# A rarely taken branch two units earlier in layer one, and another order of products in layer two's first step

## The chip, the cores and the metric

One core of one Trainium2 chip. The metric is the device time of one execution in microseconds (us); less is better. The kernel before: 1326.54 us, the median of three runs (1326.3 to 1328.52).

## The reference

Three parts, one after the other. Attention (4 batches, 8 heads, 576 tokens, 64 wide) with a threshold on the scores gives 2304 tokens of 512 values. Then "layer one", a mixture in which each token goes to one of 8 experts, and "layer two", in which each token goes through all 4 experts and the results are weighed:

```python
for e in range(E):                       # layer one, E = 8
    mask = expert_idx == e
    h = np.maximum(xe @ w1[e], 0.0)      # xe = x[mask], 512 -> 1024
    out[mask] = gate_w[mask, None] * (h @ w2[e])
for e in range(E):                       # layer two, E = 4
    h = np.maximum(x @ w1[e], 0.0)
    out += p[:, e:e + 1] * (h @ w2[e])
```

All is fp32. The kernel splits each fp32 operand into a high and a low part and makes three matmuls of the parts (high by high, high by low, low by high), which the helper `three` issues (lines 363 to 368).

## The kernel before, in words

**Layer one** (loop from line 1263) runs 72 units: nine groups of tokens (`j`), for each the four quarters of the first weights (`w == "1"`, `layer1`, line 406) and then the four of the second (`w == "2"`, `layer2`, line 418). A group has a fixed window of columns: 256 tokens of the largest expert first, then the experts by size with windows of 288, 352, 320, 288, 288, 224, 208 and 176. The last two units, 70 and 71, are the third and fourth quarter of the second weights of the last group: 24 matmuls of 176 columns each, then a copy on ACT from PSUM to `y` (line 423). Weights come by transfers on the queue of SP (`fetch`, `fetch2`), and are split into parts by ACT (high) and DVE or POOL (low).

**The branch** (lines 1319 to 1339). An expert with more tokens than its window needs more turns. `rank2` computes on the chip how many there are (`nextra`) and a table of them (`xtab`); the constants of the table, lines 211, 313 and 315, and the loop use `XW`, the columns of one turn. A first turn is made if an expert's tokens exceed its window (`th` is the window plus a multiple of `XW`, from zero up). Behind the last unit every engine loads `nextra` and branches. If there are turns, a loop does them one by one: it loads rows and weights, transposes, computes both products (2 + 8 + 4 = 14 tiles of PSUM, of which the pool `psW` has 8) and copies into `y`; behind the loop `first_part` is made again, since `y` has changed. With no turns nothing of the body runs.

**Layer two** (from line 1343) takes the 2304 tokens in three phases of 768 and makes 16 steps in each, one for a quarter of an expert's hidden columns. A step has a first product `l1` and a second `l2`. `l1` computes a 2 by 2 block product with seven products of blocks, not eight, so it needs sums and differences of blocks of the weights and of `y`. `prep1(j)` makes the weights' blocks for step j: POOL makes four sums (`sx`), `own` splits the blocks that are no sums (products 0, 1 and 2), `made` splits the sums (products 3 to 6); ACT casts the high parts, POOL subtracts for the low ones. `prep2(j)` splits the weights for `l2`. The blocks of `y` lie in parts in `yc[0]` to `yc[6]`; for the first phase `first_part` makes six of them during layer one and leaves the seventh, `yc[2]`, as values in `tt[2]`.

A product `prod(o, m)` (line 1377) is six matmuls of 384 columns, accumulated in the PSUM bank `o`; with `more` it adds to what is there. `add` is on DVE. `relu` makes the high part on ACT and returns the low part's subtraction on DVE, to be called. Within `l1` the order is

```python
prod(X, 0); p1 = copy(X); mid(); prod(Y, 4); q = Y + p1
prod(Z, 5); r = Z + q;    prod(X, 1, True); c11 = relu(0, 0, X)
prod(W, 3); c22 = W + r;  c11(); prod(Z, 2, True); relu(1, 1, c22)()
c21 = Z + q;              prod(W, 6, True); relu(1, 0, c21)(); relu(0, 1, W + q)()
```

with the sums written into PSUM banks. `mid` holds preparations for later steps. In the first step it is `first_blocks` (line 1449): the split of `yc[2]`, then `prep1(1)`'s casts, then `prep2(0)`. The blocks of step 0 (`prep1(0)`) are made at unit 70 (line 1291).

The order of work is the order of the program on each engine: the blocks are under a manual schedule, and an engine takes its instructions strictly in turn. Work of layer two that depends on nothing in the branch, such as POOL's sums for step 1, the load of the tokens' shares and the next transfer of weights, stands before the branch on its queue, since layer two is a second manual block.

Of the kernel before, what the change touches and what calls it, by code (L numbers as in the profile page):

```python
# [11 lines left out]
F32 = mybir.dt.float32  # L12
F32R = mybir.dt.float32r
# [3 lines left out]
ALU = mybir.AluOpType  # L17
# [8 lines left out]

EARLY = 256
WINDOWS = [288, 352, 320, 288, 288, 224, 208, 176]
XW = 256


@with_exitstack
def kernel(
# [309 lines left out]
    def psum():  # L343
        return pools["psum"]()
# [38 lines left out]
    def x_load(row, n, pool, tag, bufs):  # L383
        ts_ = []
        for s in range(0, n, 128):
            m = min(128, n - s)
            X = pool.tile([128, DM], F32, tag=tag, name="xrow", bufs=bufs)
            nc.sync.dma_start(X[:m, :], xs[ds(row + s, m), :])
            ts_.append((X, s, m))
        return ts_  # L390

    def x_tr(X, s, m, xT, pspool):
        ps = pspool()
        for c in range(4):
            nc.tensor.transpose(ps[:, c * 128 : c * 128 + m], in_=X[:m, c * 128 : c * 128 + 128], identity=ident[:m, :m])
        src = ps.rearrange("p (c t) -> p c t", c=4)[:, :, :m]
        nc.scalar.copy(xT[0][:, :, s : s + m], src)
        nc.vector.tensor_tensor(xT[1][:, :, s : s + m], src, xT[0][:, :, s : s + m].bitcast(F32), op=ALU.subtract)

    def x_tiles(nm):  # L400
        return [pools["m1"].tile([128, 4, max(COLS)], F32R, tag=f"x{i}", name=f"x{nm}_{i}") for i in range(2)]

    def h_tiles(nm):
        return [pools["m1"].tile([128, 8, max(COLS)], F32R, tag=f"h{i}", name=f"h{nm}_{i}") for i in range(2)]
# [33 lines left out]
    def value(ap, engines, top):  # L438
        return nc.values_load(ap, engines=engines, min_val=0, max_val=top, skip_runtime_bounds_check_because=no_need)
# [788 lines left out]
    def in_parts(m, src):  # L1228
        nc.scalar.copy(yc[m][:, 0], src)
        sub(nc.vector, yc[m][:, 1], src, yc[m][:, 0].bitcast(F32))  # L1230
# [3 lines left out]
    def first_part():  # L1234
# [20 lines left out]
        sub(nc.vector, d, b21, t4)  # L1255
        yield

    with tc.manual_schedule():
        xT, hT = early["x"], early["h"]
        ahead = first_part()  # L1260
        cols = {0: 0}
        late = iter(())
        for i in range(len(units)):
            j, w, u = units[i]
            n = COLS[j]
            if i == 0:
                for x in range(4, 8):
                    fetch(x)
                xr = x_load(eng[1] * NTOK + EARLY, COLS[1], xp, "xrow", 5)
            if i == 5:  # L1270
                for r in range(1, 8):
                    eng[r + 1] = value(tab[0:1, r : r + 1], [ET.SP], NE - 1)
            if i == 0:
                dosplit(4)
                dosplit(5, "a", "v")
            if i == 3:

                for x in range(4):
                    nc.scalar.copy(y[:, x, 0:PT], pad2.to_broadcast([128, PT]))
            if i == 2:  # L1280
                pass
            elif i > 2:
                dosplit(i + 3)
                fetch(i + 5)
            if i in (len(units) - 5, len(units) - 3):
                fetch2((i - len(units) + 5) // 2)
            if j in (4, 5) and w == "2":
                next(ahead, None)
                if j == 5:
                    next(ahead, None)  # L1290
            if i == len(units) - 2:
                prep1(0)()
            if w == "1":
                if u == 0 and j:
                    hT = h_tiles(j)
                    if j < 8:
                        xr = x_load(eng[j + 1] * NTOK, COLS[j + 1], xp, "xrow", 5)
                layer1(hls.pop(i), u, xT, n, hT, early["left"].get(i, (0, 1)))
                if i < 2 and i + 2 not in hls:
                    dosplit(i + 2)  # L1300
            else:
                if j and j not in cols:
                    a = tabE[0:1, 1:2] if j == 1 else tab[0:1, 7 + j : 8 + j]
                    cols[j] = value(a, [ET.Activation], NTOK)
                layer2(hls.pop(i), u, hT, n, cols[j])
                if u == (0 if j else 1) and j < 8:
                    xT = x_tiles(j + 1)
                    for X, s, m in xr:
                        x_tr(X, s, m, xT, psum)
            if i == 4:  # L1310
                late = rank2(*rank())
                for _ in end:
                    pass
            next(late, None)
        for _ in late:
            pass


        nextra = nc.values_load(xtab[0:1, 48:49], min_val=0, max_val=16, skip_runtime_bounds_check_because=no_need)
        with tc.If(nextra > 0):  # L1320
            with tc.For_i(0, nextra, 1) as it:
                ex = value(xtab[0:1, ds(it, 1)], [ET.SP], NE - 1)
                rx = value(xtab[0:1, ds(it + 16, 1)], [ET.SP], NTOK - XW)
                cx = value(xtab[0:1, ds(it + 32, 1)], [ET.Activation], NTOK - XW)
                xTx, hTx = x_tiles("x"), h_tiles("x")
                for X, s, m in x_load(ex * NTOK + rx, XW, xp, "xrow", 5):
                    x_tr(X, s, m, xTx, psum)
                for w in "12":
                    for u in range(4):
                        raw = w_fetch(ex, w, u, w2p.tile([128, 2, 1024], F32, tag="v2", name="rawx", bufs=2)[:, 0, :])  # L1330
                        hl = w2p.tile([128, 2, 1024], F32R, tag="v2", name="hx", bufs=2)
                        nc.scalar.copy(hl[:, 0, :], raw)
                        nc.vector.tensor_tensor(hl[:, 1, :], raw, hl[:, 0, :].bitcast(F32), op=ALU.subtract)
                        if w == "1":
                            layer1(hl, u, xTx, XW, hTx)
                        else:
                            layer2(hl, u, hTx, XW, cx)
            for _ in first_part():
                pass
    m1ctx.close()  # L1340


    with tc.tile_pool(name="m2", bufs=1) as mp, tc.manual_schedule():
# [26 lines left out]
        def l1(j, mid):  # L1370
            if j >= 3 * NS:
                return mid()
            h = hs[j] = [mp.tile([128, 2, PT], F32R, tag=f"g{x}", name=f"g{j}_{x}", bufs=2) for x in range(2)]
            wH, wL = wc.pop(j)
            X, Y, Z, W = [psum()[:, :HT] for _ in range(4)]

            def prod(o, m, more=False):
                for kk in range(2):
                    a, b_ = (wH[:, 2 * m + kk, :], wL[:, 2 * m + kk, :]), (yc[m][:, 0, kk, :], yc[m][:, 1, kk, :])
                    (aH, aL), (bH, bL) = a, b_  # L1380
                    first, last = kk == 0 and not more, kk == 1
                    nc.tensor.matmul(o, lhsT=aH, rhs=bH, start=first, stop=False, skip_group_check=True)  # L1382
                    nc.tensor.matmul(o, lhsT=aH, rhs=bL, start=False, stop=False, skip_group_check=True)  # L1383
                    nc.tensor.matmul(o, lhsT=aL, rhs=bH, start=False, stop=last, skip_group_check=True)  # L1384

            def tmp(nm):
                return mp.tile([128, HT], F32, tag=nm, name=nm)

            def add(t, a, b_):
                nc.vector.tensor_tensor(t, a, b_, op=ALU.add)  # L1390
                return t

            def relu(fc, t, src):
                o = [x[:, fc, t * HT : t * HT + HT] for x in h]
                nc.scalar.activation(o[0], src, AF.Relu)  # L1395
                return lambda: nc.vector.scalar_tensor_tensor(o[1], src, 0.0, o[0].bitcast(F32), op0=ALU.max, op1=ALU.subtract)  # L1396

            prod(X, 0)
            p1 = tmp("p1")
            nc.scalar.copy(p1, X)  # L1400
            mid()
            prod(Y, 4)
            q = add(tmp("q"), Y, p1)
            prod(Z, 5)
            r = add(tmp("r"), Z, q)
            prod(X, 1, True)
            c11 = relu(0, 0, X)
            prod(W, 3)
            c22 = add(Y, W, r)
            c11()  # L1410
            prod(Z, 2, True)
            relu(1, 1, c22)()
            c21 = add(Z, Z, q)
            prod(W, 6, True)
            relu(1, 0, c21)()
            relu(0, 1, add(W, W, q))()
# [30 lines left out]
        rest = prep1(1, True)  # L1447

        def first_blocks():
            in_parts(2, tt[2])  # L1450
            rest()
            prep2(0)

# [60 lines left out]
```

## Time and profile before

| | |
|---|---|
| median of three runs | 1326.54 us (1326.3 to 1328.52) |
| the profiled execution | 1326.68 us |
| its span, first to last instruction | 1324.6 us |
| mean granted TensorE clock | 0.995 |
| PE busy | 1301.7 us, 98% |
| POOL, DVE, ACT busy | 855.0, 843.5, 642.5 us |

All times in the rows are of the profiled execution and count from its span's start. PE is the matmul engine (PEld its weight load), DVE, ACT and POOL the vector, scalar and general engines, SP the queue of transfers; a "q" behind a name is the engine's sequencer. In a timeline, brackets give the time that the engine stood idle before the instruction and what ended it. Layer one's last unit ends and layer two begins at 571 to 573 us; `l2` of step 0 begins at 587.92.

### The profile page before, as it was taken

To read this page: it belongs to the slowest core of one execution; us is meant where nothing else is said; L and a number is where in the kernel's file an instruction comes from. 1 tells how busy PE (TensorE), PEld (TensorE's weight loads), DVE (VectorE), ACT (ScalarE), POOL (GpSimd) and SP (SyncE) were. 2 spreads that over 40 slices of the span, in tenths; PEclk is the share of its full clock that TensorE was granted. 3 is DMA by queue.
4 is the path that set the end of the run, shared out by engine and by line. 5 is a ranking of instruction groups with operands and counts; after the bars stand their busy time and mean duration, and the time that the engine had idled before them with its cause. 6 is when DMAs were issued, how large, how long until landed. Compare 5 with 4: busy or idle time off the path is not lost.

```text
span 1324.6 us, 22259 instructions
## 1 busy us (share of the span) xinstructions
PE 1301.7 (98%) x8120; PEld 1164.9 (88%) x8120; DVE 843.5 (64%) x1710; ACT 642.5 (49%) x1239; POOL 855.0 (65%) x939
## 2 busy tenths in 40 slices
PE   8999999999999999999999999999999999999997
PEld 7788887776899999999999998999999999999996
DVE  8888888887833355445555567655656675555654
ACT  7787887875554456543333334333333343333321
POOL 8876867754485443477666764777677566766642
PEclk8999999999999999999999999999999999999999
DMA  4542212002684556631122111222211122222101
GB/s 151 177 157 65 63 53 93 17 26 96 189 231 147 164 174 203 197 104 64 64 78 82 64 64 64 80 80 86 89 66 64 64 72 80 82 94 72 65 16 48
DMA packets 131537, 127.20 MB, mean 96 GB/s; under 512 B 17920, under 2 KB 110080, under 8 KB 131424
## 3 DMA queue, kind: packets, MB, share of 16 engines
q1 hardware_dynamic: 127968, 116.22, 27.8%
q0 software_dynamic: 3456, 9.51, 1.9%
q8 instruction: 66, 1.08, 0.3%
q14 instruction: 47, 0.39, 0.1%
HBM read 107.28 MB, written 18.42 MB: 95 GB/s over the span
## 4 chain that ended last, share of the span: by engine, by line
PE 53%; issue 2%; POOL 1%; ACT 0%; POOLq 0%
PE w L368 9%; PE w L366 9%; PE w L367 9%; PE w L1382 8%; PE w L1384 8%; PE w L1383 8%; POOL out_dram L192 0%; POOL v2hl L1179 0%; POOL hl L1179 0%; ACT v2hl L1218 0%; POOLq L1509 0%; POOL pad L191 0%; ACT p L1400 0%; POOLq L192 0%
## 5 line engine op out<-in xcount | busy, mean ns | idle before, releaser
L1179 POOL TENSOR_TENSOR v2hl<-raw,v2hl 128x1024 fp32r<-128x1024 f32 x48 | 116.1, 2418 | 183.6 <-ACT v2hl L1218 183.6
L1435 DVE SCALAR_TENSOR_TENSOR y<-w,big,y 128x512 f32<-128x512 f32 x252 | 184.8, 748 | 74.9 <-PE w L368 73.9
L1382 PE MATMUL w<-yc,hl 128*128 128x384 f32 x672 | 225.6, 336 | 1.4 <-ACTq L1320 0.9
L1384 PE MATMUL w<-yc,hl 128*128 128x384 f32 x672 | 225.6, 336 | 0.0
L1383 PE MATMUL w<-yc,hl 128*128 128x384 f32 x672 | 225.3, 335 | 0.0
L368 PE MATMUL w<-v2hl,g 128*128 128x512 f32 x576 | 224.8, 390 | 0.0
L366 PE MATMUL w<-v2hl,g 128*128 128x512 f32 x576 | 224.7, 390 | 0.0
L367 PE MATMUL w<-v2hl,g 128*128 128x512 f32 x576 | 224.4, 390 | 0.0
L1395 ACT ACTIVATE g<-w 128x384 fp32r<-128x384 f32 x192 | 94.5, 492 | 230.0 <-DVE w L1390 157.3
L1218 ACT CAST v2hl<-raw 128x1024 fp32r<-128x1024 f32 x48 | 50.4, 1050 | 220.1 <-PE w L368 204.3
L360 POOL TENSOR_TENSOR hl<-raw,hl 128x1024 fp32r<-128x1024 f32 x39 | 94.0, 2419 | 77.9 <-ACT hl L356 54.8
L1396 DVE SCALAR_TENSOR_TENSOR g<-w,g 128x384 fp32r<-128x384 f32 x192 | 106.7, 556 | 58.5 <-ACT g L1395 53.6
L744 POOL TENSOR_SCALAR nm<-nm,sc 128x1 f32<-128x1 f32 x144 | 93.1, 647 | 69.4 <-DVE sb L741 38.7
L761 DVE SCALAR_TENSOR_TENSOR P<-sb,nm,E 128x576 f32<-128x576 f32 x144 | 130.9, 909 | 9.7 <-ACT E L750 3.0
L1382 PEld LDWEIGHTS w<-yc,hl 128*128 128x128 f32 x672 | 126.2, 188 | 3.6 <-ACTq L1320 1.1
L368 PEld LDWEIGHTS w<-v2hl,g 128*128 128x128 f32 x576 | 108.1, 188 | 23.2
L1383 PEld LDWEIGHTS w<-yc,hl 128*128 128x128 f32 x672 | 126.2, 188 | 1.8
L367 PEld LDWEIGHTS w<-v2hl,g 128*128 128x128 f32 x576 | 108.1, 188 | 21.3
L366 PEld LDWEIGHTS w<-v2hl,g 128*128 128x128 f32 x576 | 108.2, 188 | 21.1
L1384 PEld LDWEIGHTS w<-yc,hl 128*128 128x128 f32 x672 | 126.2, 188 | 0.0
L1179 POOL TENSOR_TENSOR hl<-sx,hl 128x1024 fp32r<-128x1024 f32 x48 | 115.4, 2404 | 14.1 <-ACT hl L1194 14.1
L1179 POOL TENSOR_TENSOR hl<-raw,hl 128x512 fp32r<-128x512 f32 x96 | 97.5, 1038 | 39.6 <-ACT hl L1194 39.4
(290 smaller groups left out, 3082.9 us busy)
## 6 DMA issues: line engine op xcount, KB each, us to landing
raw<-in_moe_w_dram SPq DMA_DIRECT2D x168, 512.0 KB
xs<-zrow SPq DMA_DIRECT2D x32, 256.0 KB
kt<-in_k_dram SPq DMA_DIRECT2D x16, 256.0 KB
qt<-in_q_dram SPq DMA_DIRECT2D x16, 256.0 KB
vt<-in_v_dram SPq DMA_DIRECT2D x16, 256.0 KB
xrow<-xs SPq DMA_DIRECT2D x15, 256.0 KB
kt<-in_k_dram SPq DMA_DIRECT2D x16, 32.0 KB
qt<-in_q_dram SPq DMA_DIRECT2D x16, 32.0 KB
```

Source lines behind the costliest of these rows:

```text
L360: e.tensor_tensor(hl[:, 1, :], raw, hl[:, 0, :].bitcast(F32), op=ALU.subtract)
L366: nc.tensor.matmul(o, lhsT=aH, rhs=bH, start=first, stop=False)
L367: nc.tensor.matmul(o, lhsT=aH, rhs=bL, start=False, stop=False)
L368: nc.tensor.matmul(o, lhsT=aL, rhs=bH, start=False, stop=last)
L761: nc.vector.scalar_tensor_tensor(P, sb, nm[:, 1:2], e, op0=ALU.is_le, op1=ALU.mult, accum_out=a)
L1179: e.tensor_tensor(o, a, b_, op=ALU.subtract)
L1382: nc.tensor.matmul(o, lhsT=aH, rhs=bH, start=first, stop=False, skip_group_check=True)
L1383: nc.tensor.matmul(o, lhsT=aH, rhs=bL, start=False, stop=False, skip_group_check=True)
L1384: nc.tensor.matmul(o, lhsT=aL, rhs=bH, start=False, stop=last, skip_group_check=True)
L1395: nc.scalar.activation(o[0], src, AF.Relu)
L1396: return lambda: nc.vector.scalar_tensor_tensor(o[1], src, 0.0, o[0].bitcast(F32), op0=ALU.max, op1=ALU.subtract)
L1435: nc.vector.scalar_tensor_tensor(d, w3(o), s_, d, op0=ALU.mult, op1=ALU.add)
```

## The change

Three things. `XW` becomes 176. The branch with its loop stands before unit 70 and no longer behind unit 71; its body now keeps `x` and `h` of a turn in the tiles `yc[0]`, `yc[1]`, `yc[6]`, `yc[3]`, `yc[4]` and `yc[5]` (which `first_part` fills again behind the loop), as the tiles of the last group are still in use there. And `l1` has an order of its own for step 0, with two more PSUM banks, U and V.

```diff
-XW = 256
+XW = 176
...
+    def extra():
...
+        xt, ht = [yc[m] for m in (0, 1)], [yc[m] for m in (6, 3, 4, 5)]
+        xTx, hTx = [Parts(xt, x) for x in range(2)], [Parts(ht, x) for x in range(2)]
+        nextra = nc.values_load(xtab[0:1, 48:49], ...)
+        with tc.If(nextra > 0):
+            with tc.For_i(0, nextra, 1) as it:
...
+                        if w == "1":
+                            layer1(hl, u, xTx, XW, hTx)
+                        else:
+                            layer2(hl, u, hTx, XW, cx)
+            for _ in first_part():
+                pass
...
             n = COLS[j]
+            if i == len(units) - 2:
+                for _ in late:
+                    pass
+                extra()
...
             next(late, None)
-        for _ in late:
-            pass
-        nextra = nc.values_load(xtab[0:1, 48:49], ...)
-        with tc.If(nextra > 0):
...
+            if j == 0:
+                U, V = [psum()[:, :HT] for _ in range(2)]
+                in_parts(2, tt[2])
+                prod(X, 0)
+                p1 = tmp("p1")
+                nc.scalar.copy(p1, X)
+                prod(U, 1)
+                relu(0, 0, add(U, U, p1))()
+                mid()
+                prod(V, 2)
+                prod(Y, 4)
+                q = add(tmp("q"), Y, p1)
+                prod(Z, 5)
+                r = add(tmp("r"), Z, q)
+                c21 = add(V, V, r)
+                relu(1, 0, c21)()
+                prod(W, 3)
+                c22 = add(Y, W, r)
+                relu(1, 1, c22)()
+                prod(W, 6, True)
+                return relu(0, 1, add(W, W, q))()
...
         def first_blocks():
-            in_parts(2, tt[2])
             rest()
             prep2(0)
```

## Rows read from the trace of the kernel before

**Rows 1.** The page, part 1: busy us, share of the span, count of instructions.

```profile
PE 1301.7 (98%) x8120; PEld 1164.9 (88%) x8120; DVE 843.5 (64%) x1710; ACT 642.5 (49%) x1239; POOL 855.0 (65%) x939
```

**Rows 2.** Groups by line, PE, 588 us to the end.

```profile
L368 PE MATMUL w<-v2hl,g 128*128 128x512 f32 x576 | 224.8, 390 | 0.0
```

**Rows 3.** PE's timeline: start, duration, instruction, [idle before it and its releaser].

```profile
566.07 0.28 PE L366 MATMUL w<-h,hl 128*128 128x176 f32 x1
...
571.32 0.27 PE L368 MATMUL w<-h,hl 128*128 128x176 f32 x1
572.49 0.45 PE L1382 MATMUL w<-yc,hl 128*128 128x384 f32 x1 [0.90 <-ACTq L1320]
...
573.66 0.33 PE L1382 MATMUL w<-yc,hl 128*128 128x384 f32 x1
...
579.90 0.34 PE L1382 MATMUL w<-yc,hl 128*128 128x384 f32 x1
...
583.66 0.44 PE L1382 MATMUL w<-yc,hl 128*128 128x384 f32 x1 [0.46 <-ACT p L1400]
...
587.92 0.40 PE L366 MATMUL w<-v2hl,g 128*128 128x512 f32 x1
```

**Rows 4.** Line 1320, the engines' queues: ns min/median/max, first and last start.

```profile
L1320 ACTq EVENT_SEMAPHORE  x2: 17/17/17, 572.4 to 572.5; - x2
...
L1320 SPq COMPARE_BRANCH  x1: 50/50/50, 569.9 to 569.9; - x1
...
L1320 PEldq EVENT_SEMAPHORE  x1: 51/51/51, 571.6 to 571.6; - x1
L1320 ACTq COMPARE_BRANCH  x1: 50/50/50, 572.0 to 572.0; - x1
```

**Rows 5.** ACT's timeline.

```profile
566.47 0.93 ACT L1194 CAST hl<-raw 128x512 fp32r<-128x512 f32 x2
567.30 1.05 ACT L1194 CAST hl<-sx 128x1024 fp32r<-128x1024 f32 x1
...
571.63 0.31 ACT L423 COPY y<-w 128x176 f32 x1 [2.37 <-PE w L368]
...
581.80 0.49 ACT L1395 ACTIVATE g<-w 128x384 fp32r<-128x384 f32 x1 [1.09 <-DVE w L1390]
...
583.12 0.48 ACT L1400 COPY p<-w 128x384 f32<-128x384 f32 x1
```

**Rows 6.** POOL's timeline.

```profile
567.17 1.99 POOL L1179 TENSOR_TENSOR hl<-raw,hl 128x512 fp32r<-128x512 f32 x2 [2.65 <-ACT hl L1194]
569.12 2.38 POOL L1179 TENSOR_TENSOR hl<-sx,hl 128x1024 fp32r<-128x1024 f32 x1
...
585.64 0.74 POOL L1197 TENSOR_TENSOR sx<-raw 128x256 f32<-128x256 f32 x1
```

**Rows 7.** SP's timeline: transfers issued.

```profile
563.96 0.37 SPq L1176 DMA_DIRECT2D raw<-in_moe_w_dram  x1
569.18 0.37 SPq L1173 DMA_DIRECT2D raw<-in_moe_w_dram  x1
```

**Rows 8.** DVE's timeline.

```profile
575.15 0.96 DVE L1179 TENSOR_TENSOR yc<-t,yc 128x768 fp32r<-128x768 f32 x1 [11.21 <-ACT yc L1229]
...
576.68 0.56 DVE L1390 TENSOR_TENSOR r<-w,q 128x384 f32<-128x384 f32 x1
578.02 0.57 DVE L1390 TENSOR_TENSOR w<-w,r 128x384 f32<-128x384 f32 x1 [0.78 <-PE w L1384]
```

**Rows 9.** Stretches: length, busy us of the engines, clock, DMA share, GB/s.

```profile
6.00:9.00 3.00, 2.03 (x19) 1.78 (x20) 2.80 (x9) 1.28 (x4) 1.68 (x3) 0.80 0.45 145
9.00:12.00 3.00, 3.00 (x20) 2.80 (x18) 1.91 (x6) 2.63 (x7) 1.04 (x3) 0.50 0.78 222
...
33.00:36.00 3.00, 1.15 (x11) 0.91 (x9) 2.34 (x6) 0.80 (x5) 2.24 (x7) 1.00 0.63 185
```

**Rows 10.** Who waited for whom, PE, 24 to 40 us.

```profile
PE s L732 <- DVE sb L741: 3.5, 4, 2.5
```

More of the change, by code (lines that the diff above doesn't have):

```diff
@@ L1256, in first_part, with __init__, __getitem__ @@
         yield
+    def extra():
+        class Parts:
+            def __init__(self, tiles, x):
+                self.tiles, self.x = tiles, x
+            def __getitem__(self, key):
+                p, f, c = key
+                return self.tiles[f // 2][p, self.x, f % 2, c]
+        xt, ht = [yc[m] for m in (0, 1)], [yc[m] for m in (6, 3, 4, 5)]
+        xTx, hTx = [Parts(xt, x) for x in range(2)], [Parts(ht, x) for x in range(2)]
+        nextra = nc.values_load(xtab[0:1, 48:49], min_val=0, max_val=16, skip_runtime_bounds_check_because=no_need)
+        with tc.If(nextra > 0):
+            with tc.For_i(0, nextra, 1) as it:
+                ex = value(xtab[0:1, ds(it, 1)], [ET.SP], NE - 1)
+                rx = value(xtab[0:1, ds(it + 16, 1)], [ET.SP], NTOK - XW)
+                cx = value(xtab[0:1, ds(it + 32, 1)], [ET.Activation], NTOK - XW)
+                for X, s, m in x_load(ex * NTOK + rx, XW, xp, "xrow", 5):
+                    ps = psum()
+                    for c in range(4):
+                        nc.tensor.transpose(
+                            ps[:, c * 128 : c * 128 + m], in_=X[:m, c * 128 : c * 128 + 128], identity=ident[:m, :m]
+                        )
+                    src = ps.rearrange("p (c t) -> p c t", c=4)
+                    for c in range(2):
+                        o, i_ = [xt[c][:, x, :, s : s + m] for x in range(2)], src[:, 2 * c : 2 * c + 2, :m]
+                        nc.scalar.copy(o[0], i_)
+                        nc.vector.tensor_tensor(o[1], i_, o[0].bitcast(F32), op=ALU.subtract)
+                for w in "12":
+                    for u in range(4):
+                        raw = w_fetch(ex, w, u, w2p.tile([128, 2, 1024], F32, tag="v2", name="rawx", bufs=2)[:, 0, :])
+                        hl = w2p.tile([128, 2, 1024], F32R, tag="v2", name="hx", bufs=2)
+                        nc.scalar.copy(hl[:, 0, :], raw)
+                        nc.vector.tensor_tensor(hl[:, 1, :], raw, hl[:, 0, :].bitcast(F32), op=ALU.subtract)
+                        if w == "1":
[4 more added lines that the diff above has]
+                pass
     with tc.manual_schedule():
@@ L1314 @@
             next(late, None)
-        for _ in late:
-            pass
-        nextra = nc.values_load(xtab[0:1, 48:49], min_val=0, max_val=16, skip_runtime_bounds_check_because=no_need)
-        with tc.If(nextra > 0):
[L1321 to L1339, printed above, removed]
     m1ctx.close()
```

## The prediction, made before the changed kernel ran

> **What bounds the kernel now.** The busy shares come first: the matmul engine PE is busy for 98% of the span, every other engine for two thirds of it or less [rows 1]. So only time in which PE stands still can be won, and only time added to PE's stream can be lost. The next view, the groups by line from 588 us to the end, shows where no such time is left: none of the six matmul groups of layer two has idle time before it (one of them stands in [rows 2]). A shift that the change makes before 588 us is therefore neither made good nor made worse later, and it reaches the end at its full size.
>
> Then PE's timeline around the branch [rows 3]. The last matmul of layer one starts at 571.32 us; the last two units, 48 matmuls of 176 columns, follow each other at (571.32 - 566.07) / 47 = 0.11 us, so the next could start at 571.43. It starts at 572.49: 1.06 us lost. In layer two's first step the matmuls of 384 columns follow each other at (579.90 - 573.66) / 36 = 0.1733 us, so a product of six takes 1.04 us. The first product takes 1.17, which is 0.13 more, the price of starting anew. The second step starts at 579.90, its fourth product at 583.66 and not 18 matmuls later at 583.02: 0.64 lost. The 24 matmuls from there to 587.92 take 4.26, 0.10 more than at pitch: again the price of starting anew. From the end of layer one (571.43) to the first matmul on v2hl (587.92) there are 16.49 us, of which 84 matmuls need 14.56; the 1.93 left are these two waits, and nothing else is to be had here.
>
> What ends the two waits? The first ends with an event on ACT's queue [rows 3]. The sequencers' rows show the way there [rows 4]: PE's own event, on the far side of its branch, comes at 571.6, as soon as its last matmul is out. ACT can only come by when its last copy (571.63, [rows 5]) is out: it loads the count, branches at 572.0, and counts up at 572.4 what the body would have counted. PE starts 0.09 after that. In the program each engine with work in the body waits, on the way round it, for its own earlier work, and then adds the body's counts; PE waits for ACT's because the PSUM bank that it takes next was last used, in program order, in the body. The second wait ends with ACT's p1 copy [rows 3], which starts at 583.12: a cast of v2's weights (1.05, as at 567.30) stands before it, behind a ReLU that came late, at 581.80, at the end of DVE's chain [rows 5].
>
> **Part 1: 176 columns instead of 256.** The number enters constants of tables and the body. The table gives an expert a first turn when its tokens are more than its window, and the columns of a turn enter from the second on only, so no turn is made in either kernel. The profile has one branch for each engine (two stand in [rows 4]) and no instruction of the body. Cost 0.
>
> **Part 2: the branch two units sooner.** It removes the wait at 571.43 (1.06 + 0.13). Layer two then starts at pitch behind the last unit. But it adds the same wait before the last two units, at 566.07. PE's queue order there is unit, branch, unit; ACT's is copy of the unit's result, branch, casts. The body takes 14 PSUM tiles and there are 8 banks, so the next unit's bank was again last used in the body, and PE again waits for ACT's count, which again stands behind the copy that waits for PE's last matmul. The chain is the one seen: copy 0.20 after the end of the stream, 0.8 to the count, 0.09 to PE. I take 1.06 + 0.13, so the move is worth 0. Bounds: PE's own event stands at 571.6, so without ACT it could start near 571.9, 0.6 sooner; if ACT has more to do before the count, the nearest rows are its three casts, 1.88 (566.47 to 568.35 [rows 5]). Queued behind PE's wait are both units and layer two; behind ACT's, the casts of step 0's weights. These begin 0.8 later, and with them POOL's subtractions [rows 6], which ended at 571.5 and now end near 572.3. Step 0 starts near 572.5, so its own weights are there, and the sums, used 1.04 later in the old order and 3.1 later in the new, as well. The reorder is not needed for that. SP passes the branch when its transfers have landed: its last is issued at 563.96, and the next waits for POOL as before (569.18, [rows 7]) and is first read at 585.64 [rows 6]; some 14 us of slack hide it. POOL only loads and branches. DVE has nothing queued there: it stood idle for 11.21 us before 575.15 [rows 8].
>
> Of ACT's way the rows show 0.05 for the branch and 0.35 from there to the count [rows 4]. [...]
>
> **Part 3: the new order of step 0.** Write T for its start and count PE's stream in products of 1.04: X0 to T+1.04, U1 to 2.08, V2 to 3.13, Y4 to 4.17, Z5 to 5.21, W3 to 6.25, W6. A result is used 0.20 after the stream has passed it (571.43 to 571.63; c22 too, at 578.02, with W3 passed at 573.66 + 24 x 0.1733 = 577.82), and PE follows a reader by 0.06 (583.12 + 0.48 to 583.66) [rows 3, 5, 8]. ACT issues 0.10 before the end of the one before (566.47 + 0.93 to 567.30). Other hand-overs I take as 0.03 between ACT and DVE and 0.11 where DVE needs its own result.
> - yc2 is split first: ACT's cast follows its last copy (T+0.4 to 1.23, [rows 5]), DVE's subtraction takes 0.96 [rows 8], to T+2.2. V2's second matmul wants it at 2.25. I take 0.03, bounds 0 and 0.3.
> - mid (casts for step 1, the three of 1.88 and one of 1.05 more for v2, on ACT from T+3.3 [rows 5]) ends near T+6.1, before ACT is wanted at 6.7. Cost 0; POOL's part (4.4 us as at 567.17 and 569.12, and 2.4 for v2hl, of the size of the second, [rows 6]) ends near T+10.8, while step 1 first reads the sums at T+10.5: their part of it is done by T+8.4.
> - W6 adds to the bank that W3 wrote, and c22 must read W before. In the old order another product stood between (Z2). In the new one it does not, and c22 stands on DVE behind a longer chain. From the end of Z5: 0.20 to r, 0.56 for r, 0.11, c21 0.57, 0.03, ReLU on ACT 0.49, 0.03, its low part on DVE 0.56, less 0.09 overlap, c22 0.57, 0.06 to PE [rows 5, 8], 3.09 in all. W3 covers 1.04. So W6 waits **2.05**, and the matmuls behind it lose 0.10 as those from 583.66 did. Bounds: if c22 stood first on DVE when W3 is through, 0.20 + 0.57 + 0.06 = 0.83; with ACT 0.4 late, 2.5. All of step 1 is queued behind it; nothing overtakes on PE.
> - The wait at step 1's fourth product, 0.64 + 0.10, goes: the ReLU that is last on ACT now starts 0.8 behind W6's stream, where it was 1.9 (581.80 against 579.90, [rows 3, 5]); p1 is there about 0.5 before it is wanted. I take -0.74, bounds -0.74 and 0. Late next is then the DVE chain at W6, above.
>
> **Sum.** 0 + 0.03 + 2.05 + 0.10 - 0.74 = +1.44 us. The profiled execution took 1326.68 us (span 1324.6 and 2.08 around it), 0.14 above the median of the three runs, 1326.54. So 1326.68 + 1.44 = **1328.1**. About 0.2%, 2.7 us, is what a measurement of this kernel can tell from no change; this is 0.1%.
>
> **The rivals.**
> - *PE does not wait for ACT at the new place* (its bank comes free otherwise): 0.6 to 1.06 less, 1327.1 to 1327.5. For it: PE's own event at 571.6. Against: the count of tiles and banks.
> - *W6 finds c22 done*, since PE is held earlier or DVE comes sooner than I lay out: +1.44 - 2.15 = -0.7, 1326.0. For it: DVE does stand idle at times in step 0, 0.78 before c22 [rows 8]. Against: DVE and ACT work strictly in order, and the old trace has DVE starting r 0.7 late for just such a reason (576.68, where Z5 was passed at 575.74, [rows 8]).
> - *ACT passes the branch late* (the other side). If the three casts of step 0's weights come before the branch on ACT, its count comes 1.88 later, and PE stands that much longer: 1326.68 + 1.44 + 1.88 = 1330.0, slower by 0.25%. It decides as soon as one cast is ahead: each is on PE's path, since PE has nothing else. For it: DMA and POOL work of layer two does stand before the branch already [rows 4, 7], the issue at 569.18 with it. Against: these are in another block of the program, the casts come later in the branch's own.
> - *The clock falls* in the wait before W6. [...] Against: from 33 to 36 us PE was busy for 1.15 of 3 us, with one wait of 2.5 us [rows 10], and the clock stayed at 1.00 [rows 9]. [...]
> - *The change does not do what it says*: a turn is made after all. By the table's thresholds it cannot be.
>
> **How the numbers follow.** Forecast 0.55, no wait for ACT 0.17, c22 in time 0.12, ACT late 0.10, clock 0.03, others 0.03. The range reaches from the c22 case (1326.0) to ACT late (1330.0) and takes in the bounds of the terms. Faster by over 0.2% (below 1323.9) needs both old waits gone, no new one, and more: 0.03. Slower by over 0.2% (above 1329.2) is ACT late, the clock, and the upper bounds together: 0.15. The rest is 0.82.
>
> **What would show it.** Right: PE idle about 1.0 before the unit that started at 566.07, ended by ACT's queue; no idle time at layer two's start; idle 2 before the last product of step 0, ended by DVE's c22; none in step 1; the same stream from there, 1.5 later. Wrong: step 0 and 1 together within 15 us (part 3), or either of the last two units starting without a wait (part 2).

## The result, and the profile after

| | before | after |
|---|---|---|
| median, us (lowest to highest, runs) | 1327.07 (1326.13 to 1328.52, 6) | 1337.01 (1336.71 to 1337.9, 6) |
| the profiled execution, us | 1326.68 | 1337.01 |
| its span, us | 1324.6 | 1335.0 |
| mean granted TensorE clock | 0.995 | 0.988 |

The ratio is 1.0074, with an interval of 1.0064 to 1.0085: slower by 9.9 us. The forecast was 1328.1 with a range of 1326.0 to 1330.0, so the time lies far outside, on the side of the rivals that were slower, but beyond each of them.

The page's part 1 answers to [rows 1]: the same count of instructions on PE, and 7.0 us more of busy time, though no matmul was added.

```profile
PE 1308.7 (98%) x8120; PEld 1173.2 (88%) x8120; DVE 844.3 (63%) x1711; ACT 642.1 (48%) x1239; POOL 852.6 (64%) x939
```

PE's timeline of the kernel after, from the last matmul of unit 69 (the next could start at 567.00 + 0.11 = 567.11, by the pitch of 0.11 us from one matmul to the next) to the first of `l2` (line 1404 is what line 1382 was; it answers to [rows 3]):

```profile
567.00 0.27 PE L368 MATMUL w<-h,hl 128*128 128x176 f32 x1
570.52 0.49 PE L366 MATMUL w<-h,hl 128*128 128x176 f32 x1 [3.24 <-PEq L1271]
...
580.62 0.41 PE L368 MATMUL w<-h,hl 128*128 128x176 f32 x1
580.83 0.59 PE L1404 MATMUL w<-yc,hl 128*128 128x384 f32 x1
...
587.80 0.34 PE L1406 MATMUL w<-yc,hl 128*128 128x384 f32 x1
589.93 0.44 PE L1404 MATMUL w<-yc,hl 128*128 128x384 f32 x1 [1.79 <-DVE w L1412]
...
598.37 0.40 PE L366 MATMUL w<-v2hl,g 128*128 128x512 f32 x1
```

The wait before unit 70 is there, but it is 570.52 - 567.11 = 3.41 us and not 1.06, and what ends it is PE's own sequencer, not ACT's. Behind it units 70 and 71 take 580.83 - 570.52 = 10.31 us, where 48 matmuls at the pitch of before take 5.36. The stretches of 2 us show why (length, busy us of the engines with their counts, clock, DMA share, GB/s):

```profile
566.00:568.00 2.00, 1.28 (x12) 1.11 (x10) 0.00 (x0) 0.30 (x1) 0.00 (x0) 1.00 0.80 274
568.00:570.00 2.00, 0.00 (x0) 0.00 (x0) 0.00 (x0) 1.67 (x3) 0.97 (x1) 0.76 0.01 4
570.00:572.00 2.00, 1.48 (x7) 1.51 (x8) 0.00 (x0) 0.20 (x1) 2.00 (x3) 0.50 0.03 8
...
580.00:582.00 2.00, 2.00 (x9) 2.00 (x9) 0.00 (x0) 0.87 (x2) 0.00 (x0) 0.50 0.00 0
582.00:584.00 2.00, 2.00 (x12) 2.00 (x11) 0.96 (x1) 0.75 (x2) 0.00 (x0) 0.83 0.00 0
...
588.00:590.00 2.00, 0.21 (x2) 0.07 (x1) 1.32 (x3) 0.58 (x2) 2.00 (x1) 1.00 0.00 0
```

PE has done nothing since the last matmul of unit 69 when the granted clock falls, within 568 to 570, from 1.00 to 0.50. It stays at 0.50 through both units, in which PE works without a pause, and rises only in step 0, between 582 and 584. In the idle time before W6 (588 to 590) it stays at 1.00.

The queues' rows of the branch (line 1271; ns min/median/max, first and last start) answer to [rows 4]:

```profile
L1271 ACTq EVENT_SEMAPHORE  x2: 17/17/17, 568.1 to 568.2; - x2
...
L1271 PEldq COMPARE_BRANCH  x1: 4486/4486/4486, 565.7 to 565.7; - x1
L1271 SPq COMPARE_BRANCH  x1: 50/50/50, 565.8 to 565.8; - x1
L1271 ACTq COMPARE_BRANCH  x1: 50/50/50, 567.7 to 567.7; - x1
L1271 PEldq EVENT_SEMAPHORE  x1: 51/51/51, 570.3 to 570.3; - x1
```

ACT's count is there at 568.2, as forecast, but PE's sequencer is still in its compare-and-branch, which takes 4486 ns. The prediction had looked at this instruction's event and not at its length. In the kernel before it was already long, and stood in the same view one line from those shown:

```profile
L1320 PEldq COMPARE_BRANCH  x1: 738/738/738, 570.0 to 570.0; - x1
```

**The sum as measured**, from unit 69's end to `l2`: before 587.92 - 566.07 = 21.85, after 598.37 - 567.11 = 31.26, so 9.41 more. Of it the longer gap is 3.41 - 1.06 = 2.35; the two units at the lower clock 10.31 - 5.36 = 4.95; step 0 up to W6's wait 587.97 - 580.83 = 7.14 instead of 6.24 for 36 matmuls, 0.90, less the 0.13 of before's restart; W6's wait 589.93 - 587.97 = 1.96 and 0.12 behind it; step 1's wait, gone, -0.74. From `l2` on the streams are equal (736.7 and 736.6 us to the end). The remaining 1.04 us of the two profiled executions arose earlier, in code that is the same in both; this part varies from run to run (the same branch starts at 565.7 here and at 569.3 in the first run below).

### The profile page after: what moved, and what is told of

Same layout as the page of the kernel before. It is cut to its first block, busy times and chain, and to the rows that moved or that the text cites. A ratio compares the mean times of both kernels' runs of the same rounds, so it can differ in the third digit from the quotient of the medians.

```text
span 1335.0 us, 22259 instructions
## 1 busy us (share of the span) xinstructions
PE 1308.7 (98%) x8120; PEld 1173.2 (88%) x8120; DVE 844.3 (63%) x1711; ACT 642.1 (48%) x1239; POOL 852.6 (64%) x939
## 3 DMA queue, kind: packets, MB, share of 16 engines
q8 instruction: 66, 1.08, 0.3%
## 4 chain that ended last, share of the span: by engine, by line
PE 54%; issue 2%; POOL 1%; DVE 0%; ACT 0%; POOLq 0%
PE w L366 9%; PE w L368 9%; PE w L367 9%; PE w L1404 8%; PE w L1406 8%; PE w L1405 8%; POOL out_dram L192 0%; POOL v2hl L1179 0%; POOL hl L1179 0%; POOLq L1552 0%; ACT v2hl L1218 0%; DVE w L1412 0%; POOL pad L191 0%; DVE r L1412 0%; DVE g L1418 0%
```

## The experiments

Two questions were open: why the branch takes 4.5 us at its new place, and what the parts of the change cost alone. All ratios are to the kernel before, run beside it on the same chip (medians 1327.04 to 1327.69).

**1. The move alone.** The change with the old order of step 0:

```diff
-            if j == 0:
-                U, V = [psum()[:, :HT] for _ in range(2)]
...
-                return relu(0, 1, add(W, W, q))()
```

> The branch before unit 70 with the old order of step 0. Theory (PE's compare-and-branch has to wait for code there, 4.5 us, and the clock falls in the gap): the PE branch takes about 4.5 us again, the gap before unit 70 is about 3.4 us, the clock is at 0.5 for about 12 us, the wait before the last product of step 0 (1.96 + 0.1) is gone and the wait of 0.74 in step 1 is back: 1337.0 - 2.06 + 0.74 = 1335.7 us. Rival (the new order has a part in the long gap or in the low clock): the gap or the stretch at 0.5 becomes clearly shorter and the time falls below 1333.

Measured: 1336.02 us (1335.12 to 1339.32, 4 runs), ratio 1.0068 (1.0051 to 1.0084). PE's compare-and-branch takes 4512 ns. PE's timeline:

```profile
574.18 0.49 PE L366 MATMUL w<-h,hl 128*128 128x176 f32 x1 [3.27 <-PEq L1271]
...
596.38 0.44 PE L1404 MATMUL w<-yc,hl 128*128 128x384 f32 x1 [0.46 <-ACT p L1422]
```

The gap and the low clock (0.50 up to 586 us) come with the move, and step 1's wait of 0.46 is back. So the move alone costs 9.0 us over its kernel before, nearly all of the 9.9.

**2. The order alone.** The new order of step 0 and 176 columns, the branch in its old place:

```diff
+            if j == 0:
+                U, V = [psum()[:, :HT] for _ in range(2)]
...
+                return relu(0, 1, add(W, W, q))()
```

> The new order of step 0 and 176 columns with the branch at its old place. Theory: as the prediction's part 3 has it, the last product of step 0 waits about 2 us, the 0.74 in step 1 goes, the PE branch takes 0.74 us as before and the clock stays at 1.00: about 1.4 us over the kernel before, 1328.4. Rival (the new code alone moves the target of the branch so that it is slow): PE branch of several us and a time above 1333.

Measured: 1329.9 us (1328.42 to 1333.84, 10 runs), ratio 1.0027 (1.0017 to 1.0038); the branch takes 794 ns. PE's timeline:

```profile
572.74 0.45 PE L1382 MATMUL w<-yc,hl 128*128 128x384 f32 x1 [0.90 <-ACTq L1320]
574.95 0.34 PE L1382 MATMUL w<-yc,hl 128*128 128x384 f32 x1
575.62 0.45 PE L1383 MATMUL w<-yc,hl 128*128 128x384 f32 x1 [0.33 <-DVE yc L1179]
...
579.57 0.34 PE L1384 MATMUL w<-yc,hl 128*128 128x384 f32 x1
581.70 0.45 PE L1382 MATMUL w<-yc,hl 128*128 128x384 f32 x1 [1.79 <-DVE w L1390]
...
590.15 0.40 PE L366 MATMUL w<-v2hl,g 128*128 128x512 f32 x1
```

W6 loses 581.70 - 579.57 - 0.17 = 1.96 (forecast 2.05), V2's second matmul 575.62 - 574.95 - 0.17 = 0.50 (forecast 0.03), and there is no wait in step 1. From unit 71's end (571.68) to `l2` there are 18.47 us instead of 16.49: +1.98 where part 3 gave +1.44. This execution kept its clock (a mean of 0.998); in the two slowest of the same kernel (1332.77 and 1333.84 us) the mean granted clock was 0.991, and the median, 2.9 us above the kernel before, lies above the profile's +1.98.

**3. A short body.** If the branch's price depends on what it jumps over, a body with a quarter of its weights must be cheap (it computes a turn only in part, and no turn is made):

```diff
-                    for u in range(4):
+                    for u in range(1):
```

> The changed kernel with one quarter of the weights instead of four in the loop's body (it leaves out the other three quarters of a turn's two products, and no turn is made), so the jump over it on PE is some 300 instructions shorter. Theory (the target's code is not yet loaded because it lies far ahead): the PE branch takes under 1 us, the gap falls to about 1.1, the clock stays at 1.00, and the time is 1337.0 - 2.35 - 4.95 - 0.9 = 1328.8. Rival (the code's fetch waits behind the transfer of weights issued just before): the branch still takes 4.5 us and the time is 1337.

Measured: 1330.12 us (1328.45 to 1333.96, 8 runs), ratio 1.0022 (1.0011 to 1.0034). The branch, in its new place, takes 352 ns and the gap before unit 70 is 0.31 us (no idle time is named in its rows); from unit 70 to W6 there are 581.50 - 567.01 = 14.49 us, where the change took 589.93 - 570.52 = 19.41, so neither unit ran at the lower clock.

```profile
566.59 0.27 PE L368 MATMUL w<-h,hl 128*128 128x176 f32 x1
567.01 0.32 PE L366 MATMUL w<-h,hl 128*128 128x176 f32 x1
...
575.43 0.44 PE L1405 MATMUL w<-yc,hl 128*128 128x384 f32 x1 [0.54 <-DVE yc L1179]
581.50 0.44 PE L1404 MATMUL w<-yc,hl 128*128 128x384 f32 x1 [1.80 <-DVE w L1412]
```

The distance matters: 352 ns here, 4486 over the whole body at the same place. This body takes 5 PSUM tiles and not 14, and PE does not wait for ACT: what the first rival said, for the reason that the prediction held against it. Here the clock fell behind W6's wait: 0.50 in 582 to 584 and 0.64 in 584 to 586. The rival of the falling clock, which was given 0.03, is real at that place too, only not in every profile.

**4. The move by one unit.** The change with its branch before unit 71:

```diff
-            if i == len(units) - 2:
+            if i == len(units) - 1:
```

> The changed kernel with the branch before unit 71 instead of 70. Theory (what counts is whether the regular loading of code has reached the target): PE branches some 2.7 us later, when the next piece of code has come or is about to (568 to 569 us in both traces); branch shorter than 4.5 us, gap between 1.1 and 2.5. Rival (transfer of weights in the way): it has landed by 567.7, so the branch takes 2 to 2.5 us wherever the code lies and the gap is near 1.1. Both then give 1328 to 1331 if the clock stays up, 1335 if it falls.

Measured: 1334.13 us (1333.15 to 1335.11, 2 runs), ratio 1.0056 (1.0035 to 1.0076). The branch takes 3392 ns, the idle time behind it is 2.15 (unit 71 starts at 572.24), and the clock falls one us into unit 71 (0.82 over 572 to 574) and is 0.50 to 580. One unit is already too far.

**5. The same kernel with its code shifted.** The page's part 3 has a queue "q8 instruction" with 66 packets and 1.08 MB, so 16 KB each; 1.08 MB is 66 bytes for each of the 16240 matmuls and weight loads. That a packet is a piece of PE's code is the author's reading of these sizes; no row names the engine that it is for. Cut into windows of 0.1 us, its packets stand near the branch at 556.3 and 568.3 before, at 557.2 and 567.7 after. The next view is the count of PE's matmuls up to a moment (from the span's start; PE, then PEld). Before, at the packet and at the branch:

```profile
0.00:568.35 568.35, 554.16 (x4349) 487.39 (x4350) 393.01 (x975) 381.31 (x793) 362.02 (x516) 0.99 0.42 129
0.00:570.00 570.00, 555.81 (x4364) 489.04 (x4364) 393.01 (x975) 381.62 (x794) 363.67 (x518) 0.99 0.42 129
```

After, at the piece ahead of it, at the branch, and at the packet that came only then:

```profile
0.00:557.25 557.25, 543.29 (x4240) 477.76 (x4241) 387.78 (x968) 374.65 (x782) 354.37 (x511) 0.99 0.42 128
...
0.00:565.70 565.70, 551.74 (x4316) 486.21 (x4317) 393.18 (x975) 378.70 (x789) 359.23 (x515) 0.99 0.42 129
0.00:567.75 567.75, 553.32 (x4328) 487.63 (x4328) 393.18 (x975) 379.00 (x790) 359.23 (x515) 0.99 0.42 130
```

Before, the piece comes with the 4349th matmul, 15 matmuls ahead of the branch; with the branch 48 matmuls sooner in the program, PE is at its 4316th, and the next packet comes 2.0 us later. If that is the cause, then matmuls put far ahead, which shift the code and do nothing else, must take the price away. The change with 64 of eight columns at the kernel's start:

```diff
+        for _ in range(64):
+            nc.tensor.matmul(wm[0][:, 0, 0:8], lhsT=ones, rhs=ones[:, 0:8], start=True, stop=True)
```

> The changed kernel with 64 small matmuls (8 columns, results unused) more among the warm-up matmuls at the start: 128 instructions of PE more ahead of the branch, nothing else. Theory (PE's code comes in pieces at fixed distances; a jump is quick once the piece with its target has been in for about 2.4 us): the piece is now asked for some 7 us sooner against the branch, the PE branch takes under 0.8 us, the gap before unit 70 falls from 3.4 to about 1.1 (ended by ACT), the clock stays at 1.00 until unit 71 is through, and the wait before the last product of step 0 stays: 1337.0 - 2.35 - 4.95 - 0.9 = 1328.8, plus up to 3 at the start. Rival (transfers of weights hold the code up, or the distance alone counts): the branch takes 4.5 us and the time stays at 1337 or above.

Measured: 1330.44 us (1329.31 to 1332.33, 8 runs), ratio 1.0025 (1.0014 to 1.0036). The count at the packet of this kernel and at its branch, then its branch and PE's timeline:

```profile
0.00:562.15 562.15, 549.88 (x4349) 484.19 (x4350) 391.31 (x973) 377.50 (x788) 356.61 (x513) 0.99 0.43 129
0.00:565.60 565.60, 553.33 (x4380) 487.63 (x4381) 393.27 (x975) 378.72 (x789) 358.09 (x515) 0.99 0.43 129
```

```profile
L1273 PEldq COMPARE_BRANCH  x1: 445/445/445, 565.6 to 565.6; - x1
```

```profile
568.03 0.35 PE L366 MATMUL w<-h,hl 128*128 128x176 f32 x1 [0.90 <-ACTq L1273]
569.88 0.35 PE L367 MATMUL w<-h,hl 128*128 128x176 f32 x1 [0.15 <-issue]
...
582.46 0.44 PE L1406 MATMUL w<-yc,hl 128*128 128x384 f32 x1 [1.79 <-DVE w L1414]
```

The piece comes with the 4349th matmul again, now 31 ahead of the branch; the branch takes 445 ns, the gap is the forecast 1.06 and ends with ACT's queue, and from unit 70 to W6 there are 582.46 - 568.03 = 14.43 us (19.41 in the change), so neither unit ran at the lower clock. This was the test between the code and everything else at that place (the transfers of weights around it, the place itself): beyond the 64 matmuls themselves, only the code was moved. What is left of the loss is the order's, with the clock at 0.79, 0.50 and 0.86 over 582 to 588 behind W6's wait.

**6. A longer body at the old place.** The converse: the kernel before, with the body's loops over the weights written twice (they are never run):

```diff
-                for w in "12":
+                for w in "1212":
```

> The kernel before, branch at its old place, with the two loops of the body written twice (192 matmuls more, none of which run). Theory: the target lies one to two pieces further, its piece is not in when PE branches, so PE's compare takes about 4.5 us instead of 0.74, the gap at layer two's start becomes about 3.4 us, the clock falls, and the time is 1327.0 + 2.35 + 5 to 6 - 0.74 = about 1334. Rival (the place at unit 70 is what makes the branch slow, not the code's distance): 0.74 us and 1327.

Measured: 1331.04 us (1330.45 to 1332.81, 8 runs), ratio 1.0026 (1.0016 to 1.0036). The branch takes 4383 ns where it took 738, the gap before step 0 is 3.15 us of idle time, and the clock falls behind it.

```profile
L1320 PEldq COMPARE_BRANCH  x1: 4383/4383/4383, 571.3 to 571.3; - x1
```

```profile
576.04 0.41 PE L1382 MATMUL w<-yc,hl 128*128 128x384 f32 x1 [3.15 <-PEq L1320]
```

The code explains this too: a packet of q8 comes at 573.3, 2.0 us after the branch begins, and the branch ends 2.4 behind it. But the time is 3 us below what was expected: the clock was low for two or three stretches only (0.76, 0.50, 0.89 over 576 to 582), not through 12 us.

**7. The short body with 14 tiles.** The move with the old order, the short body, and nine transposes and copies in it, so that it takes 14 PSUM tiles again:

```diff
+                for c in range(9):
+                    ps = psum()
+                    nc.tensor.transpose(ps[:, 0:128], in_=X[:, 0:128], identity=ident)
+                    nc.scalar.copy(xt[0][:, 0, 0, 0:128], ps[:, 0:128])
...
-                    for u in range(4):
+                    for u in range(1):
```

> The branch before unit 70, the old order of step 0, and the body cut to one quarter of the weights (none of it runs; a turn's products are left out in part), but with nine transposes and copies more so that it takes 14 PSUM tiles again, not 5. Theory: the PE branch is quick (0.35 us as with the short body), but PE now waits for ACT's count as the prediction's part 2 had it, so the gap before unit 70 is about 1.06 us where the short body with 5 tiles had 0.31; no wait at W6, the 0.74 in step 1 is back, the clock stays at 1.00: the time of the kernel before, 1327.0 within 0.5. Rival (PE's wait has nothing to do with the PSUM banks): gap 0.31 and 1326.2.

Measured: 1327.77 us (1326.48 to 1328.95, 10 runs), ratio 0.9998 (0.9989 to 1.0008). The branch takes 353 ns, and PE waits for ACT again:

```profile
568.70 0.35 PE L366 MATMUL w<-h,hl 128*128 128x176 f32 x1 [0.90 <-ACTq L1271]
...
585.22 0.44 PE L1408 MATMUL w<-yc,hl 128*128 128x384 f32 x1 [0.46 <-ACT p L1426]
```

So part 2's reason for the 1.06 (the next bank was last used in the body) is shown, by 0.31 with 5 tiles and 1.07 (568.70 - 567.63) with 14.

**8. The gap without the branch.** The kernel before, in which DVE passes five more times over the low parts of unit 70's weights, so that PE waits there and no branch is moved:

```diff
+                lo = hls[i][:, 1, :]
+                for _ in range(5):
+                    nc.vector.tensor_scalar(lo, lo.bitcast(F32), 1.0, 1.0, op0=ALU.mult, op1=ALU.mult)
```

> The kernel before, branch at its old place, with DVE multiplying the low part of unit 70's weights by one, in place, five times before unit 70, so that PE has a gap of about 3.3 us there without any branch. Theory (the gap alone lets the clock fall): granted clock 0.5 from about 2 us into the gap and for about 12 us, units 70 and 71 take 10.3 us instead of 5.36, the time is 1327.0 + 3.3 + 5.9 = 1336. Rival (the branch itself, or the change of code, lets it fall): the clock stays at 1.00 and the time is 1330.3.

Measured: 1335.9 us (1335.83 and 1335.98, 2 runs), ratio 1.0061 (1.0036 to 1.0085). PE's timeline and the clock:

```profile
565.91 0.28 PE L367 MATMUL w<-h,hl 128*128 128x176 f32 x1
568.77 0.51 PE L368 MATMUL w<-h,hl 128*128 128x176 f32 x1 [2.59 <-DVEq L1324]
```

```profile
566.00:568.00 2.00, 0.18 (x2) 0.02 (x1) 1.93 (x3) 2.00 (x4) 1.10 (x1) 0.90 0.25 96
568.00:570.00 2.00, 1.23 (x6) 1.23 (x6) 0.72 (x1) 0.07 (x1) 2.00 (x3) 0.50 0.01 4
...
582.00:584.00 2.00, 2.00 (x8) 2.00 (x7) 0.60 (x1) 1.84 (x4) 0.04 (x1) 0.50 0.00 0
584.00:586.00 2.00, 2.00 (x11) 2.00 (x11) 1.38 (x3) 2.00 (x3) 2.00 (x2) 0.83 0.00 0
```

The row names DVE's own event at the branch as what ended the wait; it comes at 568.8, right behind DVE's five passes, which run from 563.58 to 568.72, so the passes set its time. PE's branch comes only at 575.5, 445 ns long. A wait of 2.6 us at this place is enough: the clock falls and comes back some 17 us later. PE's long branch is not needed for the clock's part of the loss.

**9. p1 ahead of v2's casts.** The kernel before, with step 1's `prep2` moved behind the copy of p1:

```diff
-                prep2(j + 1)
+                if j:
+                    prep2(j + 1)
...
-                l1(j + 1, lambda: None)
+                l1(j + 1, lambda: prep2(j + 1))
```

> The kernel before with one thing altered: in step 1 the casts of v2's weights stand behind the copy of p1 on ACT and no longer ahead of it (prep2(1) moves into step 1's mid). Theory (part 3's last term): the wait of 0.46 before step 1's fourth product goes, with the lost 0.18 to the pitch and 0.10 of the restart; from the end of the last unit to the first matmul on v2hl 15.75 us instead of 16.49, the time 0.7 us less than the kernel before (ratio 0.9994), clock unchanged at 0.99 or above. Rival: the DVE chain or the ReLU is late next, so the wait stays with another releaser (ratio 1.0000); or v2's weights become late for l2 of step 1 (a wait in l2, slower by up to 1 us).

Measured: 1326.76 us (1323.73 to 1332.46, 12 runs), ratio 0.9995 (0.9982 to 1.0008). In the profile the wait is gone, and from unit 71's end (572.00) to `l2` (587.76) there are 15.76 us, as expected. In the median this is too small to be told from no change.

**10. V2 between W3 and W6.** The new order with the branch in its old place, V2 three products later, and the edit of run 9 (`XW` is 176 here too, not the 256 columns that the expectation names):

```diff
-                prod(V, 2)
                 prod(Y, 4)
...
-                c21 = add(V, V, r)
-                relu(1, 0, c21)()
                 prod(W, 3)
                 c22 = add(Y, W, r)
                 relu(1, 1, c22)()
+                prod(V, 2)
+                c21 = add(V, V, r)
+                relu(1, 0, c21)()
                 prod(W, 6, True)
```

> The kernel before (branch in its old place, 256 columns) with the new order of step 0, but V2 between W3 and W6, and with step 1's casts of v2 behind p1 as in the run beside this one. Theory: W6's wait of 1.8 to 2.0 comes of W3 standing directly ahead of W6 while c22 must read W between; with V2 (1.04 us) between, c22 (done 0.83 after W3) is in time and W6 has no wait; V2 comes three products later, so its wait for the seventh block goes as well; step 1 has no wait; last unit to first matmul on v2hl 15.7 to 16.0 us against 18.47 with the order of the change, 16.49 before; the time 0.5 to 0.8 us less than the kernel before (ratio 0.9995). Rival: it is DVE's order and load that is late, then W6 waits again by 0.8 or more and the time is 1 us or more above the other run of this job.

Measured: 1326.18 us (1324.04 to 1329.09, 12 runs), ratio 0.999 (0.9978 to 1.0002). PE has one wait left, at the branch:

```profile
574.39 0.44 PE L1382 MATMUL w<-yc,hl 128*128 128x384 f32 x1 [0.90 <-ACTq L1320]
...
589.25 0.40 PE L366 MATMUL w<-v2hl,g 128*128 128x512 f32 x1
```

From unit 71's end (573.34) to `l2` there are 15.91 us. W6's 1.96 and V2's 0.50 came of the order of the products, as part 3 said of W6. This version is the lowest median of all, though its interval still touches 1.

**11. The move alone, with shifted code.** Run 1 with the 64 matmuls of run 5:

```diff
+        for _ in range(64):
+            nc.tensor.matmul(wm[0][:, 0, 0:8], lhsT=ones, rhs=ones[:, 0:8], start=True, stop=True)
...
-            if j == 0:
-                U, V = [psum()[:, :HT] for _ in range(2)]
...
-                return relu(0, 1, add(W, W, q))()
```

> Move-only (branch before unit 70, whole body, 176 columns, old order of step 0) plus 64 matmuls of eight columns at the very start, which shift PE's code by 128 instructions and do nothing else. Theory (the branch costs what the arrival of the piece of code at its target costs, and its place in the program is free): PE's compare-and-branch under 0.8 us as in the run with the shift and the new order, PE's gap before unit 70 ended by ACT with 0.90 of idle time, both last units at full clock, no wait at layer two's start, step 1's wait of 0.46 as before; the time within 0.4 us of the kernel before (ratio 1.0000), 9 us less than move-only without the shift (1336.02). Rival (the place itself costs: the distance of the jump or the transfers around it): a branch of over 3 us and 1334 to 1337 us.

Measured: 1328.34 us (1324.72 to 1333.47, 12 runs), ratio 1.0003 (0.9989 to 1.0017): 7.7 us less than run 1, and no different from the kernel before. The branch takes 445 ns. PE's timeline:

```profile
569.53 0.35 PE L366 MATMUL w<-h,hl 128*128 128x176 f32 x1 [0.90 <-ACTq L1273]
...
570.95 0.28 PE L366 MATMUL w<-h,hl 128*128 128x176 f32 x1
571.65 0.35 PE L367 MATMUL w<-h,hl 128*128 128x176 f32 x1 [0.43 <-issue]
...
586.70 0.44 PE L1406 MATMUL w<-yc,hl 128*128 128x384 f32 x1 [0.46 <-ACT p L1424]
```

The new wait inside unit 70 has no other engine as its releaser, and loses 571.65 - 570.95 - 0.11 = 0.59. A packet of q8 comes at 569.2, 2.45 us ahead of its end: most likely the piece behind the target, which the jump makes late too. The same wait costs 0.32 in run 5 (569.88; packet at 567.45).

## Why the prediction was wrong

**The step that failed is part 2's cost of the move.** It says of the new wait: "The chain is the one seen: copy 0.20 after the end of the stream, 0.8 to the count, 0.09 to PE. I take 1.06 + 0.13, so the move is worth 0", with 1.88 as the upper bound, from ACT. ACT's chain is right wherever PE's branch is short (1.05 to 1.07 in runs 5, 7 and 11). But PE has a branch too, and its cost was carried over as hidden because its event "comes at 571.6, as soon as its last matmul is out". The branch stood 12 matmuls ahead of the stream's end (4364 of 4376 before; 4316 of 4328 after), so some 1.3 us of it were covered, an estimate at the pitch of 0.11: enough for 738 ns, not for 4486.

**What sets its length**, by runs 3, 5, 6 and 11, is the arrival of code: the same jump costs 4486 ns (4512 in run 1) or, with 64 matmuls put ahead of it, 445; over the short body it costs 352, and a longer jump at the old place costs 4383. Even the 738 ns before fit: the branch ends at 570.74, 2.4 us behind the packet at 568.35; after, it ends at 570.19, 2.4 behind the one at 567.75, which itself came 2.0 us after the branch began. In run 4 the piece came 0.9 us after the branch began and the branch ended 2.4 us behind it, so its 3.4 us fit as well. The rows show when packets came and when branches ended; that a branch waits for the piece with its target is the author's reading of these times, and no row names it. PE's compare-and-branches take 352 to 4512 ns here, ACT's and SP's, before and after, 50.

**The clock** was a rival at the wrong place and at too small a chance. It was expected behind W6's wait, with 0.03. It came behind the branch's gap, and cost 4.95 + 0.90 = 5.85 us there, more than half of the loss; behind W6's wait it came in the profiles of runs 3, 4 and 5, not in those of the change and of run 2. The rows held one stretch for it, 0.80 and 0.50 over 6 to 12 us, and one against it, a wait of 2.5 us at a clock of 1.00 [rows 9, 10]; the second was given all the weight.

**Part 3** stands in its mechanism. W6's wait: forecast 2.05 and 0.10, measured 1.96 and 0.12. Step 1's wait: gone, -0.74. V2's wait was mis-sized: 0.03 (bounds 0 to 0.3), measured 0.50 in run 2 and 0.24 in run 5, with 0.11 behind it in each. DVE's subtraction on the seventh block began at T+1.44 in both, where the forecast has ACT's cast ahead of it end at T+1.23, and took 1.38 us in run 2 and 1.02 in run 5, where the row of before had 0.96 [rows 8]; why it took longer no run tells. In the kernel with the change V2 did not wait, as step 0's first products ran at the lower clock (0.50 up to 582). With V2's wait the order alone costs 1.98 and not 1.44 us in a profile that kept its clock. The rival in which c22 is in time did not come.

**Part 1** is right: no turn is made, and PE's instructions are as many as before. *ACT late* did not come: ACT's count was there at 568.2, 1.1 behind the stream's end.

**What stays open**: why the clock stays low so much longer when it falls ahead of units 70 and 71 (the change, runs 1 and 8: 13 to 17 us by the stretches' means, with PE at work without a pause for most of it) than when it falls in layer two (runs 3, 5 and 6: 3 to 4 us; run 4, ahead of unit 71 alone: 7). One more thing sets these apart: by the stretches' means the clock fell while PE stood still in the long cases, and in runs 3 to 6 only after PE had gone on, by 0.5 to 1.1 us. No run separates the two, and none tells what the chip looks at. The 2.0 us from the jump to the packet (0.9 in run 4) and the 2.4 from there to the branch's end were seen in several runs, but nothing was altered to move either.

## What to carry to other kernels

Before moving a branch that is never taken into its body, read each engine's own compare-and-branch row, the long one above all, and count on PE's instruction stream where the next piece of code comes: here a jump took 445 ns where the packet came 31 matmuls ahead of the branch (run 5), 738 where it came 15 ahead (before; the 12 matmuls still to come covered these), and 4486 where it came 2.0 us after the branch began (the change). A wait on a PE that is otherwise full is to be priced with the clock that may fall behind it: here the clock fell in waits of 2.59 us (run 8) and 3.24 (the change), and in the change it cost 5.85 us where the longer gap cost 2.35. When two products write the same bank, put another between them that covers the chain of the value read in between; here V2 between W3 and W6 took away a wait of 1.96 us (run 10).

## What the runs showed of the hardware that was not expected

- PE's compare-and-branch over a body took 352, 353, 445, 738, 794, 3392, 4383, 4486 and 4512 ns in these kernels, while ACT's and SP's took 50 in the kernel before and in the one with the change.
- Sixty-four matmuls of eight columns at the very start made the kernel with the change 6.6 us faster (medians 1337.01 and 1330.44; against the kernel beside each, 1.0074 and 1.0025); PE's branch took 445 ns and not 4486.
- An idle time of 2.6 to 3.3 us on PE was followed by 13 to 17 us at the lower clock, 0.50, where units 70 and 71 stood behind it, in most of which PE had no further wait (the change, runs 1 and 8). Behind the wait of 1.8 us before W6 the clock fell in the profiles of runs 3, 4 and 5 and stayed in those of the change and of run 2.
